# An attention layer and a 2D spectral filter on one core: first loads through GpSimd's queue and in another order, butterflies spread differently over the last projections, attention's loads regrouped

## The chip, the cores and the metric

The kernel runs on one core of a Trainium2 chip. The metric is device time in microseconds (us) from the first to the last instruction and what lies around it. Five engines work side by side, each through its own queue in order: TensorE (PE, matrix products; its weight loads are shown apart as PEld), VectorE (DVE), ScalarE (ACT), GpSimd (POOL) and SyncE (SP). A load or store is issued by one of SyncE, GpSimd or ScalarE and then moved by DMA engines that all of them share. Semaphores order the engines: an instruction that waits holds up everything behind it in its own queue.

## The reference

Two independent results are computed and laid side by side. A is causal attention in 32 heads of 18, over four segments of 512 rows, with a running memory (phi(k) v and phi(k)) that the later segments read. B is a filter in the frequency domain over a 2048 x 576 matrix.

```python
# A: x 2048 x 576, H = 32 heads of 18, N = 4 segments of L = 512
q, k, v = x @ wq, x @ wk, x @ wv                # per head and segment
for s in range(N):
    p = softmax(qs @ ks.T * 18**-0.5 + causal)
    o = g * (phi(qs) @ M) / (phi(qs) @ z + 1e-6) + (1 - g) * (p @ vs)
    M, z = M + phi(ks).T @ vs, z + sum(phi(ks))
A = concat(o) @ wo
# B
X = rfft2(x); y = irfft2(X * (w_r + 1j * w_i), s=(2048, 576))
out = concatenate([A, B], -1)
```

## The kernel before

The program has four stages, and their order on every engine is that of the Python code (`manual_schedule`): nothing is reordered by a planner, so a line's place in the loops is its place in the queue.

**Forward transform** (`FFT.forward`). B's input is cut into 16 slabs of 128 rows by 2 x 3 x 128 numbers (`xin`, 384 KB each, tile `[128,2,3,128]`). A slab goes through these steps: `load(u)` fetches it; the first half of `prep(u)` makes sum and difference of its two halves on VectorE (`eo`, L126) and their rounded high parts on ScalarE (`eh`, L129 and L130); the second half makes the low parts on VectorE (`el`, L133); `f1(u)` is 14 products with the table of cosines and sines (L145), six high by high or high by low and one for the tail, for each of two results; `ev0(u)` copies the result on ScalarE (`X`, L150), `ev1(u)` takes the difference on VectorE (L153), which also frees the product's PSUM bank (there are two); `c1(u)` is 12 products with the matrix `cfw` of that slab (L166); `evz` puts the result into `Z` (L157). The table stands in two halves, `tab[:,0]` (high parts, 580 KB) and `tab[:,1]` (low parts, 580 KB), and `tab2` (290 KB, for the tails). The table and `cfw` come through GpSimd's queue, slabs and weights through SyncE's.

The loop over u runs 20 times. In step u TensorE gets `f1(u)` and `c1(u-2)`; ScalarE gets `ev0(u-1)`, `evz(u-3)` and the casts of `prep(u+2)`; VectorE gets the sums of `prep(u+2)`, the difference `ev1(u-1)` and the low parts of the slab before. The steps 0 and 1 differ: there the first half of `prep(u+2)` comes after `ev1` and the low parts. So in step 0 slab 2's sums and casts come, and in step 1 slab 0's `ev0`, `ev1`, slab 2's low parts and slab 3's sums, in that order. From step 2 on one column block of the query and key weights is loaded, rounded and split per step (`load_w`, SyncE L442, ScalarE L446, VectorE L431), and from step 12 on the first activations of the projections (`first`, which borrows `xin`'s buffers).

Before the loop TensorE multiplies zeros (`zeros(n)`, n products of 128 x 512 numbers in bf16) that nothing reads.

**Projections** (`ATT.projections`). Four groups of 512 rows, each with nine units for queries and keys (`qk_unit`, units 0 to 8) and four for values (`v_unit`, units 9 to 12). Meanwhile VectorE does the transform's short butterflies on `Z` (`bf`, L232, and the multiplications with the filter in `middle`). `Pace` hands them out: `take(w)` adds w to a counter and issues one step for every whole number. A unit's share is its weight (1.0 for the first kind, 2.4 for the second) times the rate `tot/(sum of weights)`, where `tot` is what is left of 200 steps, less five that are kept for the stage that follows. In the last units of group 3 the first two parts of the inverse transform's input are split into high and low (`ysplit`, ScalarE L304, VectorE or GpSimd L305).

**Inverse transform** (`FFT.inverse`): 16 units of 18 products with `civ` (`i2`, L320) and 14 with the table `itab` (`i3`, L331). ScalarE and VectorE take the result of `i2` apart (L350 and L352, L357 and L358), which frees its PSUM bank. One step of the pace is taken per unit from unit 2 on. The first scores of the attention run at its end.

**Attention** (`ATT.attention`): 128 steps t, one head each, eight heads to a stack n. Step t does the maximum search of head t+11 (`s1`, L681) and the exponentials of head t (`s2`, L730 to L740), and adds up P times V (`pv`, L762) of a head group before. Beside these run the combination with the memory (`mixed`, `combine`), which needs reciprocals (`recip`: SyncE loads `ry`, stores, loads `rr` or `rd`, and TensorE spreads it, L886 and L843), and the output projection (`oproj`). Stack n+2's queries are loaded in four pieces of 384, 256, 128 and 96 KB (`stack_dmas`, L663 and L665) into one of three tiles, as keys of stack n+3 into one of four, and V of stack n+2 (`load_v`) into one of three. They stand in a list `q`, from which one is issued at the head of each step, and a second one at the end of the steps t = 8n. Stack n+2's queries are first read at step 8n+5. Stores of P times V (`u_dmas`) go through a list `qu`, two per step.

## Time and profile before

| | us |
|---|---|
| median of 3 runs | 698.64 (698.47 to 700.31) |
| the profiled execution | 696.91 |
| its span, first to last instruction | 695.2 |

| engine | busy us | share of the span | instructions |
|---|---|---|---|
| TensorE, products | 679.8 | 98% | 5040 |
| TensorE, weight loads | 503.2 | 72% | 5040 |
| VectorE | 539.0 | 78% | 1149 |
| ScalarE | 445.1 | 64% | 997 |
| GpSimd | 192.6 | 28% | 389 |

The profile is of one execution, which was 1.7 us shorter than the median. Its views are: the page (busy time, chain of waits, costliest groups), a list of waits (who waited for whom: total us, times, longest), stretches (for a stretch from A to B: its length, busy time and number of instructions of PE, PEld, DVE, ACT and POOL, granted clock of TensorE, share of the DMA engines, GB/s), timelines (start, duration, engine, line, operation, tiles out<-in, number merged, and in brackets the idle time before it and what ended it), and times of DMAs from issue to landing. An engine with a q behind its name is that engine's queue of DMA issues. A wait for several semaphores is put down to the one that came last.

### The profile page before, as it was taken

What the parts mean: (1) busy time and instruction counts of PE and PEld (TensorE: products, weight loads), DVE (VectorE), ACT (ScalarE), POOL (GpSimd) and SP (SyncE); (2) the same over time, 40 slices, a digit from 0 to 9 for tenths busy, and PEclk for the clock granted to TensorE, in tenths of its full rate; (3) what the DMA queues carried; (4) which work ended last, traced back from release to release, by engine and by line L of the source; (5) the groups of instructions that cost most, each with busy time, mean ns of one, the idle gap of its engine ahead of it and who ended that gap; (6) DMA issues with size and microseconds to landing.
All of it is one profiled execution on the core that took longest, in us unless ns stands there. A gap on an engine that the chain in (4) does not pass through costs nothing.

```text
span 695.2 us, 14377 instructions
## 1 busy us (share of the span) xinstructions
PE 679.8 (98%) x5040; PEld 503.2 (72%) x5040; DVE 539.0 (78%) x1149; ACT 445.1 (64%) x997; POOL 192.6 (28%) x389
## 2 busy tenths in 40 slices
PE   9999999999999999999999999999999999999997
PEld 6999789779779879899955455445566445673497
DVE  5998989789789679787688888888755877557633
ACT  4876794694684674454368877777766777567531
POOL 2111000100100111655235433444313653235310
PEclk9999999999999999999999999999999999999999
DMA  9995455584465778799337987986666677422142
GB/s 340 311 299 165 143 154 193 169 254 143 133 193 181 184 211 292 196 235 255 112 120 183 213 187 152 205 192 168 143 144 156 187 166 170 120 84 96 28 156 89
DMA packets 71362, 123.81 MB, mean 178 GB/s; under 512 B 12236, under 2 KB 39530, under 8 KB 67698
## 3 DMA queue, kind: packets, MB, share of 16 engines
q1 hardware_dynamic: 64638, 106.89, 57.4%
q0 software_dynamic: 5632, 15.76, 8.0%
q8 instruction: 40, 0.66, 0.4%
q10 hardware_dynamic: 1020, 0.25, 0.2%
q14 instruction: 32, 0.26, 0.1%
HBM read 82.10 MB, written 39.81 MB: 175 GB/s over the span
## 4 chain that ended last, share of the span: by engine, by line
PE 86%; DMA 4%; DVE 4%; ACT 2%; issue 2%; POOL 1%; SPq 1%; DVEq 0%; ACTq 0%; POOLq 0%
PE pj L487 15%; PE pv L762 10%; PE s L681 10%; PE pjv L487 9%; PE po L910 6%; PE i L320 5%; PE i L331 4%; PE f L145 4%; PE c L166 3%; PE s L730 3%; PE s L734 3%; PE po L939 2%; PE s L694 2%; PE pn L837 2%; DMA ux<-uD 2%
## 5 line engine op out<-in xcount | busy, mean ns | idle before, releaser
L689 DVE CUSTOM_DVE_ANT_0 junk<-s,x 128x512 bf16<-128x512 f32 x248 | 136.9, 552 | 52.7 <-PE s L681 47.0
L744 POOL TENSOR_SCALAR_AFFINE_SELECT P<-P 128x512 f32<-128x512 f32 (+2 forms) x132 | 78.9, 621 | 72.2 <-ACT P L731 70.4
L695 DVE TENSOR_REDUCE mx<-s 128x4 f32<-128x512 f32 x128 | 87.6, 684 | 4.2 <-PE s L694 1.9
L731 ACT ACTIVATE P<-s 128x512 f32<-128x512 f32 x128 | 77.8, 608 | 8.3 <-PE s L730 5.1
L762 PE MATMUL pv<-P,vs 128*32 128x512 f32 (+3 forms) x1024 | 82.2, 439 | 0.2 <-POOL P L744 0.2
L736 ACT ACTIVATE P<-s 128x512 f32<-128x512 f32 x128 | 77.6, 607 | 2.6 <-PE s L735 2.3
L740 ACT ACTIVATE P<-s 128x256 f32<-128x256 f32 x128 | 49.9, 390 | 44.9 <-PE s L739 44.6
L681 PE MATMUL s<-Ks,Qs 108*128 108x384 bf16 (+3 forms) x256 | 69.1, 301 | 2.7 <-DMA Qs<-reD 1.2
L762 PEld LDWEIGHTS pv<-P,vs 128*32 128x32 f32 x1024 | 26.7, 109 | 45.2 <-issue 35.6
L487 PE MATMUL pj<-x,wqkh 128*128 128x512 f32 x162 | 56.3, 408 | 0.0
L232 DVE TENSOR_TENSOR Z<-Z 128x580 f32<-128x580 f32 (+2 forms) x51 | 45.8, 912 | 0.5
L681 PEld LDWEIGHTS <-Qs 108*128 108x128 bf16 x320 | 31.5, 98 | 19.9 <-issue 10.0
L694 PE MATMUL s<-tri,idb 128*128 128x128 bf16 x256 | 43.0, 219 | 0.0
L320 PE MATMUL i<-civ,Y 128*128 128x256 f32 (+1 forms) x288 | 40.1, 293 | 1.8 <-ACT T L357 1.8
L545 POOL MEMSET vt<- 128x32 f32 x16 | 2.3, 162 | 138.4 <-PE pm L555 126.4
L320 PEld LDWEIGHTS i<-civ,Y 128*128 128x128 f32 (+1 forms) x288 | 37.4, 185 | 2.5 <-ACT T L357 2.0
L331 PE MATMUL i<-itab,T 128*128 128x290 f32 (+1 forms) x224 | 37.2, 310 | 0.1
L487 PE MATMUL pj<-x,wqkl 128*128 128x512 f32 x90 | 35.6, 395 | 0.0
L487 PE MATMUL pj<-xh,wqkh 128*128 128x512 f32 x90 | 35.5, 395 | 0.0
L487 PE MATMUL pj<-xh,wqkl 128*128 128x512 f32 x90 | 35.5, 395 | 0.0
L487 PEld LDWEIGHTS pj<-x,wqkh 128*128 128x128 f32 x162 | 30.4, 188 | 7.0 <-issue 0.5
L506 DVE SCALAR_TENSOR_TENSOR ex<-pj,ex 128x512 f32<-128x512 f32 (+1 forms) x28 | 19.3, 689 | 20.1 <-ACT ex L504 20.1
(216 smaller groups left out, 1809.1 us busy)
## 6 DMA issues: line engine op xcount, KB each, us to landing
qkD<-sp SPq DMA_DIRECT2D x32, 384.0 KB
xin<-xb SPq DMA_DIRECT2D x16, 384.0 KB
cfw<-cfw POOLq DMA_DIRECT2D x16, 384.0 KB, 5.2
civ<-civ POOLq DMA_DIRECT2D x16, 384.0 KB, 8.9
vs<-vD SPq DMA_DIRECT2D x16, 330.0 KB
vD<-vt SPq DMA_DIRECT2D x16, 311.0 KB
W<-w SPq DMA_DIRECT2D x16, 290.0 KB
yb<-yout SPq DMA_DIRECT2D x16, 290.0 KB
```

Source lines behind the costliest of these rows:

```text
L320: nc.tensor.matmul(p[:m,k],Y[i][:,q,c*128:c*128+m],cc[:,hl,o:o+256],start=n==0,stop=n==5)
L331: nc.tensor.matmul(p,x,t,start=n==0,stop=n==6)
L487: s.nc.tensor.matmul(out,a,b,start=i==0,stop=i==len(L)-1)
L681: nc.tensor.matmul(out,Q[:108,h,128*i:128*i+128],K[:108,h,:128*(i+1)],start=True,stop=True)
L689: nc.vector.tensor_tensor_reduce(out=junk[:,:w],in0=src,in1=s.mask[:,512-w:],scale=1.0,scalar=-3.0e38, op0=OP.add,op1=OP.max,accum_out=s.m ...
L694: nc.tensor.matmul(pa[:,o+w-128:o+w],s.idb,s.tri,start=False,stop=True,skip_group_check=True)
L695: nc.vector.tensor_reduce(out=s.mx[k][:,hh],in_=pa.rearrange("p (b c) -> p b c",c=128),axis=mybir.AxisListType.X,op=OP.max)
L731: nc.scalar.activation(P[0][:,hh],p0,AF.Exp,scale=SC)
L736: nc.scalar.activation(P[1][:,hh],p1,AF.Exp,scale=SC)
L740: nc.scalar.activation(P[2][:,hh],p2,AF.Exp,scale=SC)
L744: nc.gpsimd.affine_select(out=x[:,r],in_=x[:,r],pattern=[[0,r.stop-r.start],[1,128]],compare_op=OP.is_ge,fill=0.0,base=0,channel_multiplie ...
L762: nc.tensor.matmul(s.pvt[32*hh:32*hh+32,128*j:],vt[:,j,19*h:19*h+32],mv[0][:,hh,mv[1]],start=j==0,stop=j>1,skip_group_check=True)
```

## The change

Three places change.

First loads: slabs 1 and 2 are issued by GpSimd instead of SyncE, between the parts of the table (table's high half, slab 1, low half, tab2, slab 2, cfw 0, cfw 1); GpSimd's clearing of the attention's states and SyncE's loads of `ident` and `bm` come behind. Slabs have three buffers instead of four. Slab 0 is prepared wholly before slab 1. Slabs 3 and 4 are issued together, 4 first, which waits for slab 1's buffer; the loop's loads begin in step 1. 14 products with zeros stand before the loop instead of 26. Slab 0's 14 products take the high half of the table with high and low parts of the data first (eight products), then five zeros, then the low half, then the tail.

Butterflies: eight steps instead of five are kept for the inverse transform, and the last three units (group 3, 10 to 12) have weight 1.6 instead of 2.4.

Attention: the list `q` becomes a table by step. All four query pieces of stack n+2 are issued in step 8n, V of stack n+1 in step 8n+1, and the keys of stack n+3 in steps 8n+5, 8n+6 and 8n+7 (the last two pieces). The store list's entry comes ahead of them in the step.

```diff
-        def load(u):
-            xin[u]=xp.tile([128,2,3,128],F32,name="xin",bufs=4)
-            nc.sync.dma_start(xin[u],io["xb"][u])
+        def load(*us,eng=nc.sync):
+            for u in us: xin[u]=xp.tile([128,2,3,128],F32,name="xin",bufs=3)
+            for u in us[::-1]: eng.dma_start(xin[u],io["xb"][u])
...
-            if u==0: O.sort(key=lambda a: a[1]>1)
+            if u==0: O.sort(key=lambda a: (0,0,2,2,1,1,3)[a[1]])
...
-                if u==0 and i==3: zeros(5)
+                if u==0 and i==7: zeros(5)
...
         nc.gpsimd.dma_start(tab[:,0],io["ftab"][:,:4*FP].rearrange("p (r c f) -> p r c f",r=2,c=2))
-        late=consts()
+        load(1,eng=nc.gpsimd)
         nc.gpsimd.dma_start(tab[:,1],io["ftab"][:,4*FP:].rearrange("p (r c f) -> p r c f",r=2,c=2))
         nc.gpsimd.dma_start(tab2,io["ftab2"].rearrange("p (r f) -> p r f",r=2))
-        load(1); load(2); late()
+        load(2,eng=nc.gpsimd)
         for u in range(2): loadc(u)
-        p=[prep(u,True) for u in range(2)]
-        for i in range(2):
-            for x in p: next(x)
+        late=consts()
+        for u in range(2):
+            x=prep(u,True); next(x); next(x)
         p=[]
-        load(3)
+        load(3,4); late()
         zp=pp.tile([128,2,512],F32,name="f1",tag="f1")
-        zeros(26)
+        zeros(14)
...
-            if u+4<16: load(u+4)
-            elif u<18: next(xs,None)
+            if 0<u<12: load(u+4)
+            elif 11<u<18: next(xs,None)
...
-        P=[s.xprep(0,t,x0,xp,[128,2,3,128],"xin",4) for t in range(5)]
+        P=[s.xprep(0,t,x0,xp,[128,2,3,128],"xin",3) for t in range(5)]
...
-        tot=pace.left-5
+        tot=pace.left-8
...
-                w=tot/(35+16*2.4)*((1.0 if i<9 else 2.4) if g>0 or i>=1 else 0.0)
+                w=tot/(35+13*2.4+3*1.6)*((1.0 if i<9 else 2.4 if g<3 or i<10 else 1.6) if g>0 or i>0 else 0.0)
...
             if hh==0 and qd==0:
-                if 0<n<14: q+=s.stack_dmas(n+2,0)
-                if 0<n<13: q+=s.stack_dmas(n+3,1)
-                if n+2<16: q.insert(6,lambda n=n: s.load_v(n+2))
+                q={}
+                if 0<n<14: q[0]=s.stack_dmas(n+2,0)
+                if 0<n<15: q[1]=[lambda n=n: s.load_v(n+1)]
+                if 0<n<13:
+                    L=s.stack_dmas(n+3,1); q[5],q[6],q[7]=L[:1],L[1:2],L[2:]
...
-            if q: q.pop(0)()
             if qu: qu.pop(0)()
+            for f in q.pop(t%8,()): f()
...
-            if q and t%8==0: q.pop(0)()
             if qu: qu.pop(0)()
```

More of the change, by code (lines that the diff above doesn't have):

```diff
@@ L981, in attention @@
         m=None
-        q=[]
+        q={}
         qu=[]
@@ L996, in attention @@
             if hh==0 and qd==0:
-                if 0<n<14: q+=s.stack_dmas(n+2,0)
-                if 0<n<13: q+=s.stack_dmas(n+3,1)
-                if n+2<16: q.insert(6,lambda n=n: s.load_v(n+2))
+                q={}
+                if 0<n<14: q[0]=s.stack_dmas(n+2,0)
+                if 0<n<15: q[1]=[lambda n=n: s.load_v(n+1)]
+                if 0<n<13:
+                    L=s.stack_dmas(n+3,1); q[5],q[6],q[7]=L[:1],L[1:2],L[2:]
             st=t%32
```

## The prediction

> **What bounds the kernel now.** I read the page first (busy time, chain), then TensorE's waits, then stretches and timelines at the three places that the change touches. Rows of waits give total, times, longest.

> ```profile
> span 695.2 us, 14377 instructions
> PE 679.8 (98%) x5040; PEld 503.2 (72%) x5040; DVE 539.0 (78%) x1149; ACT 445.1 (64%) x997; POOL 192.6 (28%) x389
> ...
> PE i L320 <- ACT T L357: 1.8, 1, 1.8
> ...
> PE s L681 <- DMA Qs<-reD: 1.2, 1, 1.2
> PE s L681 <- DVE mg L689: 1.0, 1, 1.0
> ```

> TensorE works 98% of the span. So an edit is worth what it takes from TensorE's waits or from time at a lowered clock, and nothing else; a load that comes earlier than its reader needs it is worth zero. The sum is made against the profiled execution (696.91 us, span 695.2), which ran 1.7 us below the median 698.64; I take the difference over to the median.

> **First loads.** The rows are timelines of the first 18 us, then two stretches (busy time per engine, clock, DMA share, GB/s), then times from issue to landing: those of the forward table's three loads (issued at 1.32, 2.55, 3.08), those of cfw, and the big inverse table's issue row with size and median. Sizes of the others follow from their tiles: 384 KB for a slab or a cfw matrix, 580 KB for half a table, 290 KB for ftab2.

> ```profile
> 0.81 1.34 SPq L114 DMA_DIRECT2D xin<-xb  x3
> 1.26 7.14 PE L172 MATMUL f<-z 128*128 128x512 bf16 x26 [1.26 <-DVE z L170]
> 1.32 0.72 POOL L177 DMA_DIRECT2D ftab<-ftab  x1 [0.80 <-POOLq L1178]
> 3.78 1.03 DVE L126 TENSOR_TENSOR eo<-xin 128x384 f32<-128x384 f32 x2 [1.75 <-DMA xin<-xb]
> 8.06 1.03 DVE L126 TENSOR_TENSOR eo<-xin 128x384 f32<-128x384 f32 x2
> 8.79 1.25 PE L172 MATMUL f<-z 128*128 128x512 bf16 x5
> 9.76 0.40 ACT L130 CAST eh<-eo 33x256 fp32r<-33x256 f32 x1
> 12.08 0.64 ACT L150 CAST X<-f 128x580 fp32r<-128x580 f32 x1 [1.92 <-PE f L145]
> 14.30 1.96 DVE L126 TENSOR_TENSOR eo<-xin 128x384 f32<-128x384 f32 x4
> 17.98 0.80 PE L145 MATMUL f<-ftab,eh 128*128 128x290 f32 x4 [0.29 <-DVE X L153]
> 22.10 1.90 PE f L145 x14
> ...
> 0.00:6.00 6.00, 4.74 (x16) 1.92 (x17) 3.04 (x8) 2.82 (x6) 4.10 (x13) 1.00 0.72 240
> 6.00:12.00 6.00, 5.61 (x32) 3.62 (x30) 3.01 (x7) 2.28 (x6) 0.00 (x0) 1.00 1.11 385
> ...
> DMA to landing us min/median/max: 6.4/6.9/7.8
> DMA to landing us min/median/max: 3.0/5.2/12.0
> itab<-itab POOLq DMA_DIRECT2D x1, 1160.0 KB, 6.5
> ```

> The front half of the table lands at 1.32+6.4 = 7.7, and the 26 zero products hold TensorE until 8 anyway. With 14 of them (1.26+14 x 0.27 = 5.1) and a table alone at the head of its queue, slab 0's products start at about 5.9: a fixed 2.0 us (the 3.0 of a 384 KB load less 1.0 for its bytes at 385 GB/s), 580 KB = 1.5 us, and up to 1.0 us beside slab 0's own bytes. That is two microseconds, and I count it at nothing, because slab 2 takes over. ScalarE's queue holds slab 2's casts ahead of slab 0's spectrum copy. Now slab 2 is summed at 8.06, cast by 10.16, and the copy goes at 12.08, so slab 2 could come 1.92 us later, at 9.98, before anything moves. From its sum to the next (14.30) and to slab 3's products (17.98) all hangs in one chain: the copy, then VectorE's difference, slab 2's low part, slab 3's sum.

> After the change slab 2 is fifth in GpSimd's queue: 580+384+580+290+384 KB = 2.27 MB. At 385 GB/s it lands at 1.32+2.0+5.9 = 9.2; slab 0's 384 KB beside it adds up to 1.0, so 10.2. The other end is the big table's row, alone on the queue: 1160 KB in 6.5-2.0 us, 264 GB/s, which gives 11.9. I take 10.2, since the 6-to-12 stretch has the same two queues at work: +0.2 us on the chain, ends -0.8 and +1.9.

> [...]

> What the two microseconds buy is idle time: slabs 0 and 1 (2 x 1.9, and 1.25 of zeros) end near 11.2, and slab 2's products need the bank that the copy chain frees, not before 13.7. The next section shows a gap of 1.8 us followed by half clock. I expect a cut here too; 3.4 us at half would cost 1.7, but some 1.2 of it falls into the wait for slab 3's bank: +0.5, ends 0 and +1.7.

> The rest of this part is hidden. With three slab buffers instead of four each slab's load waits for one sum more, but from slab 10 on it stands behind a weight load that waits later still. The first weight loads, now behind it, have their readers three steps on. The last activation tile of the projections goes out one step later (14.30 to 17.98: 3.7 us) and is read by the last of the first unit's passes. If that cover fails, TensorE waits once at the first projection, up to 1 us; I take 0. Part: +0.7.

> **Last projections.** Stretches, then timelines around the hand-over to the inverse transform.

> ```profile
> 180.00:200.00 20.00, 19.95 (x88) 15.02 (x87) 16.44 (x24) 15.17 (x29) 2.91 (x14) 1.00 0.64 183
> ...
> 278.00:279.00 1.00, 0.00 (x0) 0.00 (x0) 1.00 (x2) 0.81 (x3) 0.92 (x2) 1.00 0.84 260
> 280.00:281.00 1.00, 1.00 (x9) 1.00 (x9) 0.97 (x2) 0.00 (x0) 1.00 (x1) 0.76 0.45 89
> 281.00:282.00 1.00, 1.00 (x6) 1.00 (x6) 0.06 (x1) 0.36 (x1) 0.92 (x3) 0.50 0.90 301
> 283.00:284.00 1.00, 1.00 (x6) 1.00 (x6) 0.43 (x1) 0.41 (x2) 0.77 (x1) 0.54 0.74 194
> ...
> 271.10 2.23 DVE L232 TENSOR_TENSOR Z<-Z 128x580 f32<-128x580 f32 x3
> 273.24 1.08 DVE L305 TENSOR_TENSOR Y<-Z,Y 128x512 fp32r<-128x512 f32 x2
> 273.31 4.42 PE L320 MATMUL i<-civ,Y 128*128 128x256 f32 x36
> 274.93 0.59 ACT L350 CAST T<-i 128x512 fp32r<-128x512 f32 x1 [0.39 <-PE i L320]
> 276.39 2.43 DVE L232 TENSOR_TENSOR t<-Z 128x580 f32<-128x580 f32 x2
> 278.74 0.68 DVE L352 TENSOR_TENSOR T<-i,T 128x512 fp32r<-128x512 f32 x1
> 279.52 3.37 PE i L320 x18
> ```

> TensorE ends its 36 products at 277.73 and starts again at 279.52: 1.79 us. The bank that it needs is freed by VectorE's L352 at 278.74. The data for that was there at 275.52 (274.93+0.59), but VectorE, full in every stretch, was still at butterflies. So the row that names ScalarE names a bystander. Then the clock stands at 0.50: 0.48 us of the stretch at 280, all of 281 and 282, 0.92 of 283, together 3.4 us, and half of that, 1.7, is lost.

> The new weights give 180/71.0 = 2.54 steps per unit of weight instead of 183/73.4 = 2.49. Stepping the generators through, units 10 to 12 of group 3 issue 13 butterflies instead of 17 (4, 4, 5 for 6, 6, 5); two more are issued before, three later. Four at 0.74 us (2.23/3) bring the split at 273.24 to 270.3, and the five behind it end near 275.1. L352 runs when its data comes, at 275.5, L358 behind it by 277.2, and TensorE at 277.73 waits for neither. GpSimd's low part of that unit is next in line, due near 278, and the fifth product, its reader, starts at 278.2. Gain 1.79+1.7 = 3.5, ends 0 and 3.5.

> The two steps issued earlier run in VectorE's idle time, 3.6 us of the 20 at 180 to 200. But there TensorE is within 0.05 us of waiting for it. A double butterfly, 1.36 us, in the wrong unit could cost up to 1.4; I take 0. The three later steps fall on units 7 to 9 of the inverse, where VectorE is off the path.

> [...]

> **Attention.** Timelines of SyncE's queue, TensorE and its weight loads.

> ```profile
> 383.28 0.37 SPq L665 DMA_DIRECT2D Qs<-reD  x1
> 390.99 0.10 PEld L681 LDWEIGHTS <-Qs 108*128 108x128 bf16 x1 [1.21 <-issue]
> 448.09 0.30 SPq L800 DMA_DIRECT2D rr<-rrD  x1
> 454.56 0.41 PE L886 MATMUL pb<-rr,sel 96*72 96x512 bf16 x1
> 556.48 0.31 SPq L807 DMA_DIRECT2D pq<-pqD  x1
> 556.83 0.37 SPq L665 DMA_DIRECT2D Qs<-reD  x1
> 564.29 0.32 PE L681 MATMUL s<-Ks,Qs 108*128 108x384 bf16 x1 [1.20 <-DMA Qs<-reD]
> ```

> The last piece of a query stack lands too late twice: issued at 383.28 for 390.99 (the wait of 0.96, in the list under DVE) and at 556.83 for 564.29. Both times a pq load of 252 KB stands in front of it. Four pieces in a row at step 8n pass it and come 0.7 us earlier by issue and some more by bytes: -2.2 at best. Against that the key pieces move from steps 3, 4, 6, 7 to 5, 6, 7, 7, right ahead of the next queries, and rr at 448.09, now second of five, becomes the fifth. Landing 7.1 us after issue, as the piece at 556.83 does, it would come at 455.6 for a reader at 454.56, on TensorE itself: +1.0. What else is queued behind the four (uD, ux, V, pq) is in no wait of TensorE's list now and is pushed back by three issues, 1.1 us. V still comes 12 steps before its reader. Part: -1.2, ends -2.2 and +2.0 (both waits kept, rr 2 us late).

> **Sum.** +0.7 -3.5 -1.2 = -4.0: profiled 692.9, median 694.6.

> **Rivals.** (1) The half clock at 280.5 has another cause than the gap. For it: the clock falls only when work has been going on for 1 us again. Against: it is the one fall inside the run, right at the longest gap. Then the hand-over is worth 1.8, and no cut comes at the start: -2.8, 695.8. (2) The hand-over wait stays because something else than VectorE's line holds it, GpSimd's low part or a transfer. For: GpSimd is full there too (0.92). Against: the times above. Then -0.5: 698.1. (3) Slower: GpSimd's queue is the limit of its own loads. Now its first 1450 KB take until 3.08+7.8 = 10.9, which is 195 GB/s from 3.3. At that rate slab 2 lands at 14.9: +4.9 and a full 1.7 of half clock, against -4.7 elsewhere: 700.5. It decides below about 234 GB/s. Against it: SyncE's queue shared the engines then, and 264 GB/s in the table's row. (4) The first loads do better: slab 2 at 9.2, no cut: -5.5, 693.1.

> **How the numbers follow.** Forecast 0.53, rival 1 0.10, 2 0.14, 3 0.08, 4 0.15. A difference under 0.3% (2.1 us) can't be told from none here. Faster: the forecast, rivals 4 and 1 but for their tails, 0.72; same: rival 2, half of 3 and tails, 0.20; slower 0.08. The range 691.8 to 698.4 leaves out rival 3 and the tails.

> **What would show it.** Right: slab 0's products before 6.5, slab 2's sum near 10.2, a gap and perhaps 0.50 before 18, slab 3's products near 18.2 to 19; no TensorE gap between 270 and 285 and no 0.50 there; no wait for Qs, a short one for rr at the first pb. Wrong: slab 2's sum after 12 or before 9.3; VectorE still behind at the hand-over; new waits of pj products at 180 to 200.

## The result, and the profile after

The changed kernel takes 701.25 us (median of 21 runs, 698.75 to 706.14) against 698.47 (21 runs, 694.92 to 705.43): the ratio is 1.0048, with a 95% interval of 1.0033 to 1.0063. It is half a per cent slower; the forecast was 694.6. The profiled execution took 703.56 us, 6.7 more than the one of before (696.91), so it shows more than the medians do; why is told below. Three single runs below took far longer than the rest of their kernel (824 us in e15, 900 in e9, 3748 in e12); ratios and clock leave them out, and without them the medians of these three would be at most 0.3 us lower.

The page of the changed kernel, its first lines:

```profile
span 701.9 us, 14350 instructions
...
PE 682.3 (97%) x5028; PEld 503.5 (72%) x5028; DVE 539.3 (77%) x1149; ACT 445.4 (63%) x997; POOL 193.1 (28%) x391
```

TensorE is busy 2.5 us longer with 12 products fewer: products at half clock count as busy (3.41 of 3.41 us in the rows at 0.50 below). The list of its own waits (total, times, longest):

```profile
PE s L681 <- DMA Qs<-reD: 2.3, 1, 2.3
PE f L145 <- DVE X L153: 2.1, 1, 2.1
PE pb L886 <- DMA rr<-rrD: 1.9, 1, 1.9
...
PE f L145 <- DMA ftab<-ftab: 1.2, 1, 1.2
...
PE pj L516 <- ACT sp L514: 0.6, 2, 0.3
```

`PE i L320 <- ACT T L357` with its 1.8 us is gone, as forecast. In its place stand a wait ahead of slab 2's products (L145), one for rr, and the query wait, which grew from 1.2 to 2.3. Stretches of the same execution, chosen so that each pair is one window of 3.41 us and the one behind it:

```profile
14.08:17.49 3.41, 1.23 (x7) 0.95 (x7) 2.05 (x4) 1.28 (x3) 0.00 (x0) 1.00 0.96 331
17.49:20.90 3.41, 3.41 (x17) 3.41 (x16) 2.51 (x6) 2.69 (x5) 0.00 (x0) 0.50 0.56 187
454.40:457.81 3.41, 1.55 (x23) 0.77 (x16) 1.06 (x4) 0.47 (x2) 1.19 (x2) 1.00 0.81 146
457.81:461.22 3.41, 3.41 (x17) 1.81 (x15) 3.28 (x11) 2.44 (x6) 0.11 (x1) 0.50 0.32 104
567.04:570.45 3.41, 1.23 (x12) 0.74 (x16) 1.19 (x5) 1.82 (x6) 3.33 (x7) 1.00 0.94 201
570.45:573.86 3.41, 3.41 (x22) 1.23 (x18) 1.22 (x5) 0.69 (x3) 0.72 (x2) 0.50 0.87 214
270.00:280.00 10.00, 10.00 (x81) 10.00 (x80) 8.39 (x14) 3.81 (x10) 0.51 (x6) 1.00 0.81 282
280.00:285.00 5.00, 4.91 (x40) 4.70 (x39) 2.43 (x5) 3.87 (x10) 4.80 (x7) 1.00 0.56 149
```

Three stretches of half clock (0.50), each right behind a window in which TensorE was busy 1.23 to 1.55 us of 3.41; each costs 1.7 us (half of 3.41). The execution of before had one, at 280.51. None is left at the hand-over (last two rows).

How much later the same product of TensorE starts than before, followed through the two traces: +3.3 us at 60 us, +2.4 at 225, +3.5 at 268, +0.3 at 300, +0.4 at 445, +3.9 at 458, +6.4 at 568, +6.5 at the end. So the first loads cost 3.3 (1.7 of it half clock), 0.9 came back between 60 and 225 (0.6 of it by 85, as in e2, which has the second part alone), group 3 of the projections cost 1.0, the hand-over gave back 3.1, and attention lost 6 in two places, 3.4 of it half clock.

### The profile page after: what moved, and what is told of

Read it like the earlier page. It is cut to its first block, busy times and chain, and to the rows that moved or that the text cites. A ratio compares the mean times of both kernels' runs of the same rounds, so it can differ in the third digit from the quotient of the medians.

```text
span 701.9 us, 14350 instructions
## 1 busy us (share of the span) xinstructions
PE 682.3 (97%) x5028; PEld 503.5 (72%) x5028; DVE 539.3 (77%) x1149; ACT 445.4 (63%) x997; POOL 193.1 (28%) x391
## 4 chain that ended last, share of the span: by engine, by line
PE 83%; DMA 7%; ACT 3%; DVE 3%; issue 2%; POOL 1%; SPq 1%; ACTq 0%; POOLq 0%; DVEq 0%
PE pj L487 14%; PE s L681 9%; PE pv L762 9%; PE pjv L487 8%; PE po L910 6%; PE i L320 4%; PE i L331 4%; PE f L145 4%; PE c L166 4%; PE s L730 3%; PE s L734 3%; PE po L939 2%; PE s L694 2%; PE pn L837 2%; PE s L739 2%
## 5 line engine op out<-in xcount | busy, mean ns | idle before, releaser
L689 DVE CUSTOM_DVE_ANT_0 junk<-s,x 128x512 bf16<-128x512 f32 x248 | 136.9, 552 | 53.4 <-PE s L681 47.9
L681 PE MATMUL s<-Ks,Qs 108*128 108x384 bf16 (+3 forms) x256 | 69.8, 304 | 3.9 <-DMA Qs<-reD 2.3
L681 PEld LDWEIGHTS <-Qs 108*128 108x128 bf16 x320 | 31.8, 99 | 22.9 <-issue 9.6
L232 DVE TENSOR_TENSOR Z<-Z 128x580 f32<-128x580 f32 (+2 forms) x51 | 45.9, 913 | 0.6
L320 PE MATMUL i<-civ,Y 128*128 128x256 f32 (+1 forms) x288 | 39.2, 288 | 0.1
L320 PEld LDWEIGHTS i<-civ,Y 128*128 128x128 f32 (+1 forms) x288 | 36.6, 181 | 0.8 <-POOL Y L305 0.3
L681 PE MATMUL s<-Ks,x 108*128 108x384 bf16 (+3 forms) x128 | 34.6, 300 | 0.2
```

The costliest lines, as they stand in the source:

```text
L320: nc.tensor.matmul(p[:m,k],Y[i][:,q,c*128:c*128+m],cc[:,hl,o:o+256],start=n==0,stop=n==5)
L681: nc.tensor.matmul(out,Q[:108,h,128*i:128*i+128],K[:108,h,:128*(i+1)],start=True,stop=True)
L689: nc.vector.tensor_tensor_reduce(out=junk[:,:w],in0=src,in1=s.mask[:,512-w:],scale=1.0,scalar=-3.0e38, op0=OP.add,op1=OP.max,accum_out=s.m ...
```

## The experiments

All times are medians; the ratio is to runs of the kernel before on the same chip. "Clock" is the mean over a kernel's runs of its span times one minus its granted clock: what was lost to the clock (half clock behind the last product counts in it too, 0.8 us in the profile of before). For the kernel before that is 1.02 us over 114 runs; 66 of these had a granted clock of 0.999 or more and a median of 696.76, the other 48 one of 699.51. (In e13 one record of 0.949, in a run that took no longer than the rest, is left out of the mean.)

| run | us | before | ratio (95%) | clock, us |
|---|---|---|---|---|
| the change | 701.25 | 698.47 | 1.0048 (1.0033 to 1.0063) | 3.27 |
| e1 first part | 700.79 | 697.98 | 1.0045 (1.0024 to 1.0066) | 1.93 |
| e2 second part | 695.82 | 697.98 | 0.9962 (0.9942 to 0.9982) | 0.23 |
| e3 third part | 702.49 | 697.98 | 1.0067 (1.0043 to 1.0091) | 2.52 |
| e4 slabs 3, 4 behind | 702.04 | 697.98 | 1.0056 (1.0036 to 1.0076) | 3.21 |
| e5 nothing behind slab 2 | 703.43 | 697.57 | 1.0071 (1.0046 to 1.0096) | 3.61 |
| e6 slab 2 on SyncE | 699.71 | 697.57 | 1.0020 (1.0004 to 1.0037) | 1.57 |
| e7 keys back | 699.23 | 697.57 | 1.0018 (1.0001 to 1.0035) | 0.93 |
| e8 keys back, rr earlier | 699.94 | 697.57 | 1.0024 (1.0007 to 1.0041) | 0.87 |
| e9 smaller second part | 696.35 | 697.01 | 0.9985 (0.9966 to 1.0004) | 0.63 |
| e10 gap filled | 699.65 | 697.01 | 1.0026 (1.0007 to 1.0044) | 1.28 |
| e12 e9, query piece earlier | 694.80 | 697.01 | 0.9948 (0.9928 to 0.9968) | 0.28 |
| e13 e7, store on GpSimd | 699.62 | 699.09 | 1.0004 (0.9984 to 1.0023) | 1.52 |
| e14 e12, store on GpSimd | 694.56 | 699.09 | 0.9931 (0.9909 to 0.9953) | 0.23 |
| e15 store on GpSimd alone | 698.71 | 699.09 | 0.9996 (0.9976 to 1.0017) | 1.46 |

**The three parts alone.** e1, e2 and e3 are the kernel before with the hunks of one part of the diff each.

> The kernel before with the change's first part alone (first loads by need, 14 and 5 zero products, three slab buffers). Theory A (slab 2 comes late, because the load that SyncE issues as soon as slab 0's buffer is free shares the engines with it): the lag of the changed kernel between 85 and 206 us, 2.4 to 2.8, is the whole price of this part: 2.6 us slower than before, slab 2's sum again at 12.4 to 12.8, slab 3's products near 21.5 instead of 18. Rival B (the lag in that stretch comes from elsewhere, as the extra half-clock stretch at 17.5 that one execution has and others need not have): under 1 us slower.

> The kernel before with the second part alone (thinner butterflies at the last projections). Theory A: the wait at the hand-over and its half clock go (3.1 to 3.5 us, as in the changed kernel, where the lag fell from 3.46 to 0.32), and some 1.0 us comes back in group 3, where the changed kernel's lag grew from 2.43 at 206 to 3.47 at 258: 2.3 us faster, 1.8 to 3.5. Rival B (that growth in group 3 has nothing to do with the butterflies): 3.3 to 3.5 us faster, and no new TensorE waits at 240 to 255. Rival C (the half clock was not caused by the gap): 1.8 us faster at most, with a half-clock stretch still near 280.

> The kernel before with the third part alone (attention's loads by need). Theory A (rr's load stands behind four query pieces, and the keys right ahead of the queries delay these): a wait for rr of 1.5 to 2.0 us at the first pb product of group 0, near 453, and a longer query wait near 563 (2.0 to 2.4 for 1.2), each with a half-clock stretch behind it where it is long enough: 2.0 us slower by the waits alone, 3 to 5.5 with the half clock. Rival B (those two waits are there only because the work before came 3 us later): under 1 us slower, or faster by up to 1.2 as predicted.

e1: 2.8 slower, as theory A has it in time and place; its cause, slab 4 on SyncE, is for e4 and e5. Slab 2's sum again at 12.61 (VectorE's timeline), the wait ahead of its products 2.26 us:

```profile
12.61 1.03 DVE L126 TENSOR_TENSOR eo<-xin 128x384 f32<-128x384 f32 x2 [1.80 <-DMA xin<-xb]
```

e2: 2.2 faster, theory A. No wait at the hand-over, no half clock, but two new waits in group 3 that the kernel before does not have (TensorE's timeline); the same pair stands in the changed kernel at 248.72 and 252.64. Between 245 and 258 the lag grows by 0.9 us. By 85 us it had fallen by 0.6: a wait of 0.43 at 83 is gone.

```profile
246.05 0.38 PE L516 MATMUL pj<-sp,nid 128*128 128x512 bf16 x1 [0.33 <-ACT sp L514]
...
249.97 0.38 PE L516 MATMUL pj<-sp,nid 128*128 128x512 bf16 x1 [0.29 <-ACT sp L514]
```

e3: 4.5 slower, theory A; rival B falls, since the waits are there without the other parts (TensorE's timeline):

```profile
406.36 0.32 PE L681 MATMUL s<-Ks,Qs 108*128 108x384 bf16 x1 [1.36 <-DMA uD<-U]
...
456.43 0.38 PE L886 MATMUL pb<-rr,sel 96*72 96x512 bf16 x1 [1.84 <-DMA rr<-rrD]
...
567.59 0.32 PE L681 MATMUL s<-Ks,Qs 108*128 108x384 bf16 x1 [2.66 <-DMA uD<-U]
```

The two L681 rows are query waits: the profile names uD, which landed at about the same time, but these products read the queries, whose last piece landed at 406.01 and 567.29. The three add up to 2.8 - 2.2 + 4.5 = 5.1 against 2.8 for all together; the intervals (about 0.37% on the sum of the ratios) allow that.

**The first loads.** Three kernels change who stands behind or beside slab 2, one looks at the head of the queue.

e4, the first part with slabs 3 and 4 behind:

```diff
             x=prep(u,True); next(x); next(x)
+            load(3+u,eng=nc.gpsimd)
...
-        load(3,4); late()
+        late()
```

> The first part alone, but slabs 3 and 4 go on GpSimd's queue behind slab 2 and the first two weight loads, slab 3 first; SyncE issues no slab between slab 0 and slab 5. Theory A (slab 4, which the changed kernel issues on SyncE at 4.94 us, takes slab 2's place): slab 2 lands near 10.8 (between 10.4 and 11.1: 930 KB that are left at 8.0 us, at 300 to 385 GB/s), its sum near 10.9, and this kernel is 0.5 to 1.2 us slower than before, some 1.7 better than the first part as it was. Rival B (GpSimd's queue alone is the limit): slab 2's sum still after 12.2 and 2.6 us slower.

4.1 slower, and slab 2's sum at 12.29, after theory A's 11.1. But the edit did one thing more: SyncE's two small constants, which had stood behind slab 4, went out at 1.27 and 1.73 instead of 9.6 and later, and the table's front half landed at 8.03 instead of 7.17 (e1). So e4 alone does not clear slab 4; e5, where the constants come late again, does.

```profile
12.29 1.03 DVE L126 TENSOR_TENSOR eo<-xin 128x384 f32<-128x384 f32 x2 [0.63 <-DMA xin<-xb]
```

e5 holds everything behind slab 2:

```diff
+        hold=xp.tile([128,4],F32,name="hold",bufs=1)
+        nc.gpsimd.tensor_copy(hold,xin[2][:,0,0,:4])
+        load(3,eng=nc.gpsimd)
         for u in range(2): loadc(u)
+        load(4,eng=nc.gpsimd)
```

> The first part alone, but nothing is issued behind slab 2 until it has landed: GpSimd waits for it with a copy of four columns, and only then issues slab 3, the first two weight loads and slab 4; SyncE issues no slab between slab 0 and slab 5, and the two small constants come later. Theory A (loads overlap: engines that are through with their share of slab 2 go on to the weight loads behind it, and that traffic takes the bandwidth from the engines that are late): slab 2 lands at 10.4 to 11.0 us instead of 12.3 to 12.6, its sum follows at once, the wait of TensorE ahead of slab 2's products falls from 2.2 to at most 1.0, and the kernel is 0.3 to 1.3 us slower than before instead of 2.8. Rival B (some of the engines are slow with this queue whatever stands behind): slab 2 still after 12.0, 2.5 us slower or more.

```profile
11.65 1.03 DVE L126 TENSOR_TENSOR eo<-xin 128x384 f32<-128x384 f32 x2 [0.48 <-DMA xin<-xb]
```

Slab 2's sum at 11.65, with nothing behind or beside it: so slab 4 falls as the whole cause. What stands behind and beside slab 2 costs about 1 us (12.61 less 11.65), and 1.4 of the 2.4 that my 10.2 was short is the queue itself. These are single profiles (that of e5 is of its longest run, 709.53, of which only the start is read here). In the trace 2.3 MB of the queue had moved by 10.5 us in e4, as much as all loads up to slab 2, but slab 2 was whole only at 12.27. The time of the kernel (5.9 slower) says nothing on this, since slabs 3 and 4 and cfw then came late (waits of 0.94 and 2.70 us at 18.7 and 23.2).

e6 puts slab 2 back on SyncE:

```diff
-        load(0)
+        load(0); load(2)
...
-        load(2,eng=nc.gpsimd)
```

> The first part alone, but slab 2 goes on SyncE's queue right behind slab 0, as before; the table's halves, slab 1 and the weights stay on GpSimd's queue in the new order. Theory A (all of the first part's loss is slab 2 behind the table in GpSimd's queue): slab 2 lands before 6.5 us, the wait ahead of its products falls under 1.0 us, and the kernel is within 0.7 us of before. Rival B (the loss comes from the last quarter of the table and slab 1, which start later there): TensorE still waits 1 us or more before 12 us and over 1.5 us before 18, 2 us or more slower.

2.1 slower by the medians, 1.4 by the ratio, and between the theories again. Slab 2 landed at 5.07, its products wait 0.58 us instead of 2.26; but then TensorE waits 0.81 us for the table's front half (until 7.91), 0.63 for the low half (10.95) and 0.54 at 19.6. The lag at 20 us is 1.6 where e1 has 3.2, so in the traces half of the part's loss goes with slab 2; the other half stays with the new order of the other loads. The times are not as sharp: of 2.8 by the medians 2.1 stay, of 3.1 by the ratios 1.4.

e11 lets the front half go alone:

```diff
+        hold=xp.tile([128,4],F32,name="hold",bufs=1)
+        nc.gpsimd.tensor_copy(hold,tab[:,0,0,0,:4].bitcast(F32))
         load(1,eng=nc.gpsimd)
```

> The first part alone, but GpSimd issues slab 1 and all that follows only when the table's front half has landed. One look at that landing; what comes later is late on purpose. Theory A (loads behind the front half take the engines before it is through: 580 KB of that queue were moved by 5.8 us in the first part alone, but the front half landed at 7.2): it lands between 5.0 and 6.2 us. Rival B (some engines are late with the first load itself): 6.6 us or later.

It landed at 6.54, 5.2 us after its issue, against 5.7 in the changed kernel and 5.8 in e1; by the numbers neither theory, but nearer to B. In the trace its first bytes moved at 3.1, 500 of the 580 KB by 5.5, and the rest took until 6.5, with nothing else on its queue; SyncE's slab 0 was whole at 3.93 (one profiled run). Times from issue to landing of the table's three loads, first of the changed kernel, then of e11 (the least is the front half):

```profile
DMA to landing us min/median/max: 5.7/7.0/8.5
```

```profile
DMA to landing us min/median/max: 5.2/5.2/5.4
```

So being first in GpSimd's queue does not give 2.0 us plus bytes at 385 GB/s (3.5); alone on it, 580 KB took 5.2.

**The projections.** e9 keeps the pace of the kernel before up to unit 9 of group 3:

```diff
-                w=tot/(35+16*2.4)*((1.0 if i<9 else 2.4) if g>0 or i>=1 else 0.0)
+                w=tot/(35+16*2.4)*((1.0 if i<9 else 2.4 if g<3 or i<10 else 1.6) if g>0 or i>=1 else 0.0)
```

> The second part in a smaller form: the weights of the last three units of group 3 are 1.6 as in the change, but all units before them keep the pace of the kernel before (tot and divisor as before), so no butterfly moves before unit 10 and about six more steps than before are left for the inverse. Theory A (the 0.9 us that the second part loses at 245 to 258 comes from double butterflies that the higher pace puts into other units): no wait of TensorE over 0.25 us between 230 and 260, none at the hand-over, and 2.6 to 3.6 us faster than before, against 2.1 for the second part as it was. Rival B (the steps left over are paid in the inverse): new waits between 285 and 345, not faster than the second part as it was.

The trace is as theory A has it: no wait between 230 and 260, none at the hand-over, and the steps left over are free in the inverse (VectorE 34.56 busy of 40 where it was 31.02, TensorE full):

```profile
236.00:246.00 10.00, 10.00 (x46) 7.56 (x44) 8.26 (x10) 7.82 (x16) 0.33 (x2) 1.00 0.89 237
246.00:256.00 10.00, 10.00 (x45) 7.78 (x45) 6.97 (x10) 8.39 (x21) 0.00 (x0) 1.00 0.79 214
...
300.00:340.00 40.00, 40.00 (x320) 37.71 (x319) 34.56 (x86) 17.04 (x43) 21.78 (x33) 1.00 1.03 219
```

The time is not: 696.35, where e2 has 695.82, and the intervals overlap. The 0.9 us at 245 to 258 come from the pace, but taking them away is not seen in the median. 0.4 us of that stand in the clock's column (0.63 for 0.23 in e2); the rest is not explained.

**Is it the gap that brings the half clock?** e10 fills it:

```diff
+            if u==2:
+                p=pp.tile([128,512],F32,name="idle",tag="mt")
+                for _ in range(12): nc.tensor.matmul(p[:,:128],*s.fill,start=True,stop=True)
```

> The kernel before with twelve products of 128 columns, whose result nobody reads, on TensorE right ahead of the product that waits at the hand-over (1.3 us in the gap of 1.8). The wait stays as long as it is; only TensorE is not idle in it. Theory A (a stretch of half clock follows when TensorE stood idle for about 1.8 us within one window of 3.4 us, so the gap of 1.79 us costs its 1.7 us in only some of the executions): no half clock between 270 and 290, the same start of the 18 products after the gap, the time lost to the clock falls from 1.0 us in the mean to under 0.5, and the kernel is 0.3 to 1.2 us faster than before. Rival B (the half clock has nothing to do with the gap): a half-clock stretch near 280 in as many executions as before, 0 to 0.5 us slower.

```profile
278.23 0.84 PE L348 MATMUL idle<-tri,idb 128*128 128x128 bf16 x12
280.08 2.13 PE L320 MATMUL i<-civ,Y 128*128 128x256 f32 x16 [1.01 <-ACT T L360]
...
391.43 0.32 PE L684 MATMUL s<-x,Qs 108*128 108x384 bf16 x1 [2.31 <-DMA Qs<-reD]
```

The wait lasts 1.7 us as ever, and with 0.7 of it filled no half clock follows, as theory A has it. This one profile does not decide, though: of the eleven profiles in which the hand-over is that of the kernel before, six have the half clock behind it and five (e3, e4, e8, e11, e15) have none. What speaks against rival B is e2, with no gap there and 0.23 us lost to the clock in the mean, and the table at the end. Theory A's number for the time falls: 2.6 slower by the medians, 1.8 by the ratio. TensorE came to the query products at 389.11, 0.95 earlier than before, but the queries landed at 391.34, 0.4 later than before (390.93): the wait grew from 0.96 to 2.31, and now this gap has the half clock behind it (stretches of e10).

```profile
388.97:392.38 3.41, 1.09 (x10) 0.60 (x8) 1.46 (x6) 2.05 (x6) 1.33 (x4) 1.00 0.90 165
392.38:395.80 3.42, 3.42 (x23) 1.23 (x22) 1.38 (x5) 1.17 (x4) 1.64 (x2) 0.50 0.93 247
```

In e15, whose profile has no half clock at the hand-over either, TensorE also came 1.07 earlier and waited 1.87 for the same queries.

**Attention.** e7 takes the keys back to where they were, e8 also moves rr ahead:

```diff
-                    L=s.stack_dmas(n+3,1); q[5],q[6],q[7]=L[:1],L[1:2],L[2:]
+                    L=s.stack_dmas(n+3,1); q[3],q[4],q[6],q[7]=L[:1],L[1:2],L[2:3],L[3:]
...
-                    r=s.recip(s.rD[g-1],s.rrD[g-1],s.g1,False,"rr",2)
+                    r=s.recip(s.rD[g-1],s.rrD[g-1],s.g1,False,"rr",1)
```

> The third part alone, but the key pieces go out at steps 3, 4, 6 and 7 of eight again instead of 5, 6, 7 and 7. Theory A (the keys right ahead of the queries made the query waits long; rr's wait comes from the four query pieces alone): the query waits near 404 and 565 fall from 1.4 and 2.7 us to under 0.8 each, the wait for rr near 455 stays at 1.6 to 2.0: 0.3 us faster to 1.5 slower than before. Rival B (the place of the keys does not matter): a query wait of 2 us or more stays and the kernel is 3 us or more slower.

> As the run with the keys back, and the reciprocal's write and read (rrD, rr) one step earlier, so that rr stands ahead of the query pieces. Theory A: the wait for rr goes (under 0.3 us) as well: 0.5 to 1.7 us faster than before. Rival B (rr comes late because its data are late, not because of the queue): a wait for rr of 1 us or more stays, no faster than before.

e7: 1.7 slower, 1.2 by the ratio, against 4.5 with the keys moved. No query wait is left at 404 or 565. At 565 none is left in e8 and e13 either, which have the keys in the same place, so there the keys made it. At 404 it is only covered in e7 (queries whole at 407.07, their first product at 407.42): the same product waits 0.81 in e8 and 1.16 in e13. The wait for rr, expected to stay, does not show: rr lands at 459.25 for a product at 459.29, which other delays had held back by then. e8: no wait for rr, which lands at 452.69 for a reader at 454.41; but 2.4 slower, so theory A's time falls. For rr's wait it has another, the longest that TensorE has in attention (TensorE's timeline of e8):

```profile
405.40 0.32 PE L681 MATMUL s<-Ks,Qs 108*128 108x384 bf16 x1 [0.81 <-DMA pq<-pqD]
...
458.07 0.32 PE L681 MATMUL s<-x,Qs 108*128 108x384 bf16 x1 [1.60 <-DVE mg L689]
```

Both are the first products to read a stack of queries, whose last pieces landed at 405.04 and 457.77; the second stack now stands behind rr. Another kind of wait is new. e7, timelines of ScalarE and of TensorE:

```profile
411.74 0.39 ACT L740 ACTIVATE P<-s 128x256 f32<-128x256 f32 x1
414.13 0.65 ACTq L720 DMA_DIRECT2D Qs<-mts  x1
414.82 0.60 ACT L731 ACTIVATE P<-s 128x512 f32<-128x512 f32 x1 [2.69 <-PE s L694]
```

```profile
415.47 0.38 PE L730 MATMUL s<-Qs,x 110*128 110x512 bf16 x1 [1.09 <-ACT P L731]
```

ScalarE stands from 412.13 to 414.13 before it issues a small store: it waits for a semaphore which a key piece of SyncE (issued at 407.62, landed at 414.05) still holds. In the traces the issues of SyncE and ScalarE use eight semaphores in turn (108 and 112 to 118 in the changed kernel), and this one waited for the load eight issues back (0.08 us from its landing to the issue). Moving loads moves who waits for whom. In e8 the same happens at 411, 466 and 571 (1.1 to 1.6 us), each time within 0.1 us of the landing of the load eight issues back.

e13 and e15 let GpSimd issue that store, in e7 and in the kernel before:

```diff
-        else: s.later(2,lambda: nc.scalar.dma_start(out,mt))
+        else: s.later(2,lambda: nc.gpsimd.dma_start(out,mt))
```

> As the run with the keys back (third part, keys at steps 3, 4, 6, 7), but the small store of the row maxima (Qs<-mts, L720) is issued by GpSimd instead of ScalarE. Theory A (with the query waits gone, that kernel is still slower because ScalarE stands at this issue until an earlier load has landed, 2.0 us at 414, and the exponentials behind it come late): no wait of ScalarE over 1 us there, no wait of TensorE over 0.8 us at 399 to 418, and 0.2 to 1.2 us faster than before, where the run with the keys back was 1.7 slower. Rival B (the loss has another place, GpSimd's masks come late instead): still 1 us or more slower.

> The kernel before with nothing but this store on GpSimd. Theory A (in the kernel before ScalarE hardly waits at this issue, so nothing is to be had): within 0.5 us of before. Rival B (GpSimd's issue, 0.5 to 0.6 us each time, delays the masks): 1 us or more slower.

e15 is level, so the store by itself is worth nothing that these runs can tell. e13 is level too: by the ratios about 1.0 us better than e7, though the intervals overlap, with no wait of TensorE at 411 to 418. But one of 1.16 at 407 is there, which the profile puts down to VectorE and whose product reads queries that were whole only at 407.58, and now rr's wait shows (1.23 at 457.19), which e7's delays had covered. So ScalarE's issue is behind the wait at 415, and probably part of e7's loss; theory A's gain over before was too much.

e12 moves the last query piece, and with it what stands behind it in the list, one step earlier, in e9; e14 adds the store on GpSimd:

```diff
-            if q and t%8==0: q.pop(0)()
+            if q and t%8<2: q.pop(0)()
```

> The second part in its smaller form, and in attention only one edit: the last query piece goes out in the second step of eight instead of the third (two pieces in each of the first two steps), and all behind it one step earlier; the reciprocal's loads and the order of the rest stay as before. Theory A (only the last query piece is late, and a small move is enough): the two query waits of 0.96 and 1.20 us fall to 0.5 or less each, 0.5 to 1.5 us faster than the run with the smaller second part alone. Rival B (every move in that queue brings another wait, on a later load or on ScalarE's own issue, as the run with the keys back showed): not faster than that run, with a new wait of 0.5 us or more in attention.

> The fastest run so far (smaller second part, last query piece one step earlier) with the same store on GpSimd. Theory A: its waits of 0.58 and 0.3 us at 411 to 414 go, 0.3 to 1.2 us faster than that run, 2.5 to 3.5 faster than before. Rival B (GpSimd's masks come late): no faster than that run, new waits of the pv products.

e12 is 2.2 faster than before, 1.5 better than e9 by the medians (the intervals of the ratios just meet): both query waits are gone (under 0.25 us), and one of 0.58 at 411 is new, so each theory has a part. e14 (six runs) has 694.56, 4.5 faster than before and more than was expected; by the ratios it is 1.2 better than e12, but their intervals overlap; the waits at 411 to 414 are gone, and one of 0.46 at 403 is new. In both no gap after 20 us is over 1.03 us, and every run of them had a granted clock of 0.999 or more. These are the fastest versions: e14 is 0.7% faster than the kernel before, and 1.2% faster than the changed one if both are set against it.

## Why the prediction was wrong

**First loads: +0.7, measured +2.8 (e1).** The step that failed is "at 385 GB/s it lands at 9.2": it treats GpSimd's queue as one pipe that delivers loads in order at the rate of the whole. From its first byte to 8 us the queue moved 270 to 310 GB/s, later loads took part before earlier ones were whole (with slab 4 beside them, 1 us by e5), and the table's front half took 5.2 us even alone on the queue (e11). Slab 2's sum came at 12.63, neither 10.2 nor rival 3's 14.9. Even the upper end of my bounds for the landing, 11.9, from a load that was alone on the queue, was too low. Rival 3 has about the time, 700.5, but by luck: its rate of 195 GB/s is not one that the queue had. The half clock behind the new gap was mis-sized too: +0.5 in the sum, since 1.2 of it was to fall into a wait; in e1 no wait stands behind it, and 1.7 of the lag of 3.2 is from it (in the mean over its runs e1 loses 0.9 more to the clock than the kernel before). Two smaller steps failed as well. The 14 zero products ended at 7.40, not 5.1: 0.27 us each is the mean of the 26 of before, of which the first seven started 0.40 to 0.43 apart and the later ones 0.22; in the changed kernel's profile all 14 started 0.40 to 0.43 apart. So in this run slab 0 could not start at 5.9 whatever the table did:

```profile
1.26 6.14 PE L172 MATMUL f<-z 128*128 128x512 bf16 x14 [1.26 <-DVE z L170]
7.16 0.83 PE L145 MATMUL f<-ftab,eh 128*128 128x290 f32 x4
...
11.69 0.54 PE L145 MATMUL f<-ftab,el 99*128 99x290 f32 x2 [1.22 <-DMA ftab<-ftab]
...
16.25 0.81 PE L145 MATMUL f<-ftab,eh 128*128 128x290 f32 x4 [2.12 <-DVE X L153]
```

And the description of the change said that slab 4 waits for slab 1's buffer. It got slab 0's: SyncE's first load behind slab 0 went out at 4.94, just as slab 0's sums ended (4.91). What that cost is at most a part of the 1 us that e5 gives for all that stands behind and beside slab 2. The chain itself (sum, casts, copy, difference, bank) held: sum at 12.63, products at 16.25, 3.6 us later.

**Last projections: -3.5, measured -2.2 (e2).** The mechanism was right, row by row: thirteen butterflies, L352 waits for its data and not for VectorE, no gap, no half clock at the hand-over, and rival 2 falls. Two sizes were off. The 1.7 us of half clock were counted whole, but the kernel before loses them only in some runs: its mean is 1.02 for all causes, e2's 0.23, so this was worth 0.8. And the steps that I counted at nothing ("a double butterfly in the wrong unit could cost up to 1.4; I take 0") cost 0.9, in group 3 at 245 to 258, not at 180 to 200; 0.6 of it came back by 85 us, which the sum had not either.

**Attention: -1.2, measured +4.5 (e3).** The sign was wrong, and two steps did it. "Four pieces in a row pass pq and come earlier: -2.2" left out the keys, of which I had said that they move right ahead of the queries, and priced them for rr alone; where the sum had the two waits of 0.96 and 1.20 gone, e3 has three, of 0.61, 1.36 (of another stack, which did not wait before) and 2.66. With the keys back both old waits are gone in e7, e8 and e13, as the -2.2 had it, but the new one at 405 to 408 is not (0.81 in e8, 1.16 in e13); what makes it stays open. "rr +1.0" had the right cause and half the size: 1.84. And nothing in this part of the sum stood for the half clock behind new gaps: e3 loses 2.52 us to the clock where the kernel before loses 1.02.

**The rivals.** Rival 1 (another cause for the half clock) falls with e2, which has neither gap nor half clock there, and with the table below; e10 fits. In the traces gaps of 1.8 to 2.3 us were followed by it (1.78 in the kernel before, 2.31 in e10). The range ended at 698.4, although the bad ends of the three parts together (+3.6, 0 and +2.0) would have given 704.2, and the clock was counted at two places only: at the hand-over, where it was seen, and at the start.

## What to carry to other kernels

When a profile shows a stall that is followed by half clock, ask first how often that happens: price it by the mean granted clock over many runs, not by the one trace, and price every gap that a change may open in the same way. A load is not moved alone: write down what stands ahead of it in its queue after the move, for the moved ones and for those that they pass, and what waits at the issue itself. Small moves (one query piece and what follows it one step earlier, three weights, in e14 a store's issuer) gave 0.5 to 0.7% here; regrouping whole queues lost it.

## What the runs showed of the hardware

| idle in one window, us | windows | followed by a window at half clock |
|---|---|---|
| 1.86 to 2.67 | 11 | 11 |
| 1.78 to 1.84 | 5 | 3 |
| 1.30 to 1.65 | 14 | 1 |
| less | the rest | 0 |

A long gap that falls across a border can pass: e3's of 2.66 us was split into 1.14 and 1.52, and the clock stayed at 1.00 (stretches of e3):

```profile
562.66:566.07 3.41, 2.27 (x14) 1.04 (x11) 2.71 (x9) 3.41 (x9) 2.24 (x2) 1.00 0.94 145
566.07:569.48 3.41, 1.89 (x16) 0.88 (x20) 1.30 (x3) 1.37 (x4) 2.97 (x7) 1.00 0.98 263
569.48:572.89 3.41, 3.35 (x33) 1.84 (x26) 2.38 (x7) 2.16 (x6) 0.00 (x0) 1.00 0.89 226
```

At the unchanged hand-over gaps of 2.40 (e4) and 2.53 (e11) passed in this way, and one of 1.77 (e7) did not. That explains why the same kernel has runs with and without the loss, as far as the profiled runs show.

**Loads of one GpSimd queue overlap, and the last part comes late** (e4: 2.3 MB moved by 10.5 us, slab 2 whole at 12.27). In the changed kernel's trace the semaphore of slab 2 rose in sixteen steps from 10.05 to 12.61, and that of cfw 0, the load behind it, from 11.65 on. What makes the last steps late the traces do not show, and what makes e11's 5.2 us stays open.

**An issue on ScalarE can stop its arithmetic**: 2.0 us in e7, for a load that another engine had issued 6.5 us earlier.
